# 67 of 367 transfers joined, and the planner's boxes of 16-bit tiles mended, in a two-layer spectral kernel

## The chip, the core and the metric

The kernel runs on one core of one Trainium2 chip. The metric is the device time of one execution in microseconds (us); the time before is the median of three runs. Engines are named as in the profile: PE (matrix multiply), PEld (its weight load), DVE (vector), ACT (scalar and activation), POOL (GpSimd), SP (issues transfers). SPq and ACTq are the issues of transfers by SP and ACT.

## The reference

x is one sequence of 2048 rows of 512 numbers. Four steps are added to it in turn, each on the layer-normalized x: layer A, layer B, layer A, layer B.

```
x = x + _A_ref(_layernorm(x, axis=-1), A_w_r, A_w_i)
x = x + _B_ref(_layernorm(x, axis=-1), B_A_re, ..., B_Dskip)
x = x + _A_ref(_layernorm(x, axis=-1), A_w_r, A_w_i)
x = x + _B_ref(_layernorm(x, axis=-1), B_A_re, ..., B_Dskip)
```

Layer A is a two-dimensional real Fourier transform over rows and columns, a product with a complex weight for each frequency, and the inverse transform. Layer B convolves every column with its own kernel of 2048 taps, by transforms of length 4096, and adds x times Dskip. The kernel of layer B is K[d, l] = Re sum over n of C B dt exp(dt A l), for 512 columns d and 128 states n; it depends on the parameters alone and is the same in both layers B.

## The kernel before, in words

Everything is float32 in matmuls, apart from bfloat16 factors for the exponentials. All transforms are written as small dense matmuls in two or three steps, with twiddle tables from the host. x (128 x 16 x 512) stays in SBUF, and large fixed areas (`Y`, `Ya`, `wk`, `apart`) are cut into rings of tiles by hand; a ring's line gives the number of columns and of tiles, `"KT": (512, 4)` for instance.

The work falls into two parts, each with a list of its own. The first part holds the first layer A (`forward_a`, `first_a` for 16 groups of frequencies, `inv_a` for 16 row blocks), the making of layer B's kernel K (`load_k`, `exp_k`, `unit_k` for 32 units, `store_k` for four quarters q), and the kernel's spectrum. That spectrum has two steps. `turn_k(q, i)` reads a piece of K back from the DRAM list `kd`, multiplies it with `cRk` (L1253) and stores both halves to the DRAM list `yk` (L1274, issued by ACT). `spectra_k(q)` reads `yk` (L837) with a table `cGk` (L834), multiplies (the matmuls of `spectrum`, L826), copies on ACT (L846) and stores to the DRAM list `khat` (L847, issued by ACT). It makes the first 256 of the 512 columns; the other 256 are made in the second part inside `group_b` (L898 reads `yk`, L907 stores `khat`), with blocks of the table that `load_g` loads (L866).

The second part holds the rest of the first layer B (`forward_b`, `group_b` for eight pairs of frequency groups and two column halves e, `inv_b`), the second layer A (`first_a` once, `group_a` 15 times) and the second layer B. The last quarter of K (q = 3) is turned here, from tiles of the rings `yk` and `gk` that `load_t` holds for it until its four turns are stored.

While `first_a` runs in the first part, its tables stand in x's own place (ring `G`, five tiles), so `inv_a` loads x's rows anew from DRAM (L732), as soon as all 16 groups are done.

What sets the order. Each piece of work is a generator. It yields what it needs next (an engine, tiles of a ring, the time of an event), and `Clock.run` takes the piece that can go first by planned times, ties by a rank written by hand. The planned times come from a cost table `COST` and from transfers' bytes through one rate; a planned instruction waits for earlier ones whose boxes (partitions and columns in a tensor) it meets. `Clock.boxes` works these boxes out. For a tile viewed as bfloat16 it counts the columns in 16-bit elements and leaves them so, though they are compared with columns of float32 tiles. Each engine then works off its own instructions in exactly this order; real waits are semaphores, put in from the real addresses.

Transfers go through two queues, SP's and ACT's. The built program has eight completion semaphores for them and gives them out in turn over the merged order of both queues. So that a semaphore is never in use twice, a transfer is issued only when the one eight places ahead has landed; the engine that issues it stands still until then.

```
yield "SP KT KT gb", self.after(("turn", 0), 8)
...
for j in range(2):
    nc.scalar.copy(kh[j].rearrange("p r d -> p (r d)"), p[j])
    nc.scalar.dma_start(self.khat[:, 2 * q + j, :, :256], kh[j])
```

The two loads of a table and of its weights stand next to each other at L595 and L597 (`group_a`) and at L667 and L669 (`first_a`); the products with the table are L623 and L685, those with the weights are on DVE.

Of the kernel before, what the change touches and what calls it, by code (L numbers as in the profile page):

```python
# [10 lines left out]
AF = mybir.ActivationFunctionType  # L11
OP = mybir.AluOpType

RING1 = {"yd": (1024, 5), "oh": (1280, 1), "KS": (2048, 1), "KT": (512, 4), "yh": (512, 4), "gb": (256, 3), "st": (256, 2), "sk": (128, 1)}
# [31 lines left out]
WORK = 17664  # L46
# [149 lines left out]
class Clock:  # L196
# [51 lines left out]
    @staticmethod  # L248
    def boxes(ap):

        if str(ap.space) == str(DRAM):
            return [(0, 1, 1, ap.offset, 1, ap.offset + sum(a * (b - 1) for a, b in ap.ap) + 1)]
        (s, n), *rest = ap.ap
        size = mybir.dt.size(ap.dtype) / mybir.dt.size(ap.tensor.dtype)
        width = round(int(np.prod(ap.tensor.shape[1:])) / size)
        p, o = divmod(ap.offset, width)
        rest = sorted(((a, b) for a, b in rest if b > 1 and a), key=lambda d: -abs(d[0]))
        o += sum(a * (b - 1) for a, b in rest if a < 0)
        rest = [(abs(a), b) for a, b in rest]
# [142 lines left out]
class Net:  # L402
# [185 lines left out]
    def group_a(self, g):  # L588

        nc = self.nc  # L590
# [4 lines left out]
        nc.sync.dma_start(ca, self.io["cGa"][g])  # L595
        W = G[:, 768:1796].rearrange("p (r s f) -> p r s f", r=2, s=2)
        nc.sync.dma_start(G[:, 768:1798], self.io["W"][g])  # L597
# [62 lines left out]
    def first_a(self, r, g):  # L660

        nc = self.nc
# [63 lines left out]
    def inv_a(self, r, s2, st):  # L726

        nc = self.nc
        xs = self.x[:, s2, :]
        yield "SP" if not r else "PE", self.after(("group", r), 16)  # L730
        if not r:
            nc.sync.dma_start(xs, self.io["A_x"].rearrange("b (p s) d -> p (b s) d", p=128)[:, s2, :])  # L732
            self.mark("again", s2)
            yield "+"
        yield "PE p:t y"
        Y4 = self.w("y", [128, 512])
# [25 lines left out]
        q = self.psum("h")  # L762
        nc.tensor.matmul(q, self.RaT, Y4, start=True, stop=True)
        self.drop(Y4)
        yield "DVE" if r else ("DVE", self.after(("again", s2)))

        two = xs.rearrange("p (a b) -> p a b", a=2)
        nc.vector.tensor_tensor(two, two, q[:, None, :256].to_broadcast([128, 2, 256]), op=OP.add)
# [60 lines left out]
    def spectra_k(self, q):  # L829

        nc = self.nc
        yield "SP KT KT gb", self.after(("turn", 0), 8)
        gb = self.w("gb", [128, 2, 4, 32])
        nc.sync.dma_start(gb, self.io["cGk"][q])  # L834
# [3 lines left out]
        yield "PE p:k yh yh"  # L838
        kh = [self.w("yh", [128, 2, 256]) for _ in range(2)]
        p = self.psum("k")  # L840
        p = p[:, :512], p[:, 512:]
        self.spectrum(gb, y, p)
        self.drop(gb, *y)
        yield "ACT"
        for j in range(2):
            nc.scalar.copy(kh[j].rearrange("p r d -> p (r d)"), p[j])  # L846
            nc.scalar.dma_start(self.khat[:, 2 * q + j, :, :256], kh[j])  # L847
        self.mark("khat", q)

    def tables(self, r):  # L850
# [7 lines left out]
            self.nc.sync.dma_start(self.gi[r, q], self.io["cGb"][q])  # L858
            self.mark("gi", r, q)

    def load_g(self, q):

        yield "SP gk", self.emitted(("rows", 0, 1), 8)
        gk = self.gk[q] = self.w("gk", [128, 2, 4, 32])
        self.timer.keep(gk)
        self.nc.sync.dma_start(gk, self.io["cGk"][q])  # L866
        self.mark("gk")
        yield self.emitted("gk", q + 1)

    def early(self, q):  # L870

# [337 lines left out]
    def load_t(self):  # L1209
# [11 lines left out]
        nc.sync.dma_start(self.sk3, self.io["B_Dskip"].rearrange("(q a d) -> q a d", q=4, a=1)[3])  # L1221
        self.mark("last")

    def turn_k(self, q, i):

        nc = self.nc
        kd = self.kd[q].rearrange("j (a s) d -> a j (s d)", s=16)
        last = q == 3
        if last:
            yield self.emitted("last")  # L1230
            KT = self.KT3[:, :, 128 * i:128 * i + 128]
        else:
            yield "SP KT", self.after(("stored", q))
            KT = self.w("KT", [128, 4, 128])
            nc.sync.dma_start(KT, kd[:, :, 128 * i:128 * i + 128])
        if i == 0:
            if last:
                sk = self.sk3
            else:
                yield "SP sk"  # L1240
                sk = self.w("sk", [1, 128])
                nc.sync.dma_start(sk, self.io["B_Dskip"].rearrange("(q a d) -> q a d", q=4, a=1)[q])
            yield ("DVE", self.after("last")) if last else "DVE"
            o = KT[0:1, :, 0:32]
            nc.vector.tensor_tensor(o, o, sk.rearrange("p (j d) -> p j d", j=4), op=OP.add)
        yield ("PE p:x p:x", self.after("last")) if last else "PE p:k"
        if last:
            p = [self.psum("x") for _ in range(2)]
        else:
            p = self.psum("k")  # L1250
            p = p[:, :512], p[:, 512:]
        for h in range(2):
            nc.tensor.matmul(p[h], self.Rk[:, h, :], KT if last else KT.rearrange("p j m -> p (j m)"), start=True, stop=True)  # L1253
        if not last:
            self.drop(KT)
        for h in range(2):
            if not last:
                yield "ACT yh"
                r = self.w("yh", [128, 4, 128])
            elif not h:  # L1260
                yield "ACT"
                r = KT
            else:
                yield "DVE"
                r = self.wk[:, self.own[2].offset % WORK + 512 * i:][:, :512].rearrange("p (s d) -> p s d", s=4)
            out, in_ = r.rearrange("p s (j d) -> p s j d", j=4), p[h].rearrange("p (j s d) -> p s j d", j=4, s=4)
            if last and h:
                nc.vector.tensor_copy(out, in_)
# [5 lines left out]
            nc.scalar.dma_start(self.yk[q // 2, :, :, :, i, h, 128 * (q % 2):128 * (q % 2) + 128]  # L1274
                                .rearrange("g c a d -> (g c) a d"), r)
            if not last:
                self.drop(r)
            yield "+"
        self.mark("turn", q // 2)
        if last:  # L1280
            self.left -= 1
            if not self.left:
                self.drop(*self.own)

    def plan_k(self):

        M, KS = {}, {}
        self.F, self.th = self.w("F", [128, 2, 2, 512]), self.w("th", [128, 512])
        self.hi = [self.w("hi", [128, 1024]).bitcast(BF).rearrange("p (a r m) -> p a r m", a=2, r=2) for p in range(3)]
        yield -130, self.setup_b()  # L1290
        yield -110, self.setup_a()
        for a in range(2):
            for r in range(2):
                yield -105, self.setup_f(a, r)
        for b in range(8):
            yield 4 * b - 2, self.load_k(b)
            for n in range(6):
                yield 4 * b - 1, self.exp_k(b, n, M)
            for u in range(4 * b, 4 * b + 4):
                yield u, self.unit_k(u, M, KS)  # L1300
# [87 lines left out]
    def plan_rest(self, sb):  # L1388
# [100 lines left out]
```

## Time and profile before

| | |
|---|---|
| median of 3 runs | 803.64 us (803.43 to 808.02) |
| the profiled execution | 801.81 us |
| its span, first to last instruction | 800.0 us |
| mean granted PE clock | 0.944 |
| transfers issued | 367 |

A line of the waits reads "who <- for whom: us in total, times, longest". A line of a timeline reads "start, length, engine, line, operation, output <- input, count", with the engine's idle time ahead of it and who ended it in brackets. A wait is put down to the event that came last. "L826" is line 826 of the kernel before. Tensors have the program's names without numbers, so a tile of a ring shows as the area that it is cut from (`wk`, `Y`, `Ya`, `x`).

### The profile page before, as it was taken

To read this page: it belongs to the slowest core of one execution; us is meant where nothing else is said; L and a number is where in the kernel's file an instruction comes from. 1 tells how busy PE (TensorE), PEld (TensorE's weight loads), DVE (VectorE), ACT (ScalarE), POOL (GpSimd) and SP (SyncE) were. 2 spreads that over 40 slices of the span, in tenths; PEclk is the share of its full clock that TensorE was granted. 3 is DMA by queue.
4 is the path that set the end of the run, shared out by engine and by line. 5 is a ranking of instruction groups with operands and counts; after the bars stand their busy time and mean duration, and the time that the engine had idled before them with its cause. 6 is when DMAs were issued, how large, how long until landed. Compare 5 with 4: busy or idle time off the path is not lost. (4 is left out here: it accounts for less than half of the span.)

```text
span 800.0 us, 23463 instructions
## 1 busy us (share of the span) xinstructions
PE 648.6 (81%) x9892; PEld 419.3 (52%) x9892; DVE 510.2 (64%) x1022; ACT 419.5 (52%) x767; POOL 306.5 (38%) x339
## 2 busy tenths in 40 slices
PE   4389888967899799888858887889887898788796
PEld 4377555535456344346423453777665554444465
DVE  5975667747748594885525454886767588466532
ACT  5765898886886957845232324175533233433130
POOL 4290336516425340320314325264544554075420
PEclk9699999997999999999898999999997999999999
DMA  9217212630624668547986783940664524866839
GB/s 325 60 59 274 89 47 84 192 96 14 217 80 151 233 205 244 181 133 165 259 219 194 193 246 131 255 174 1 232 218 139 186 56 107 186 195 160 257 89 281
DMA packets 85960, 132.51 MB, mean 166 GB/s; under 512 B 5756, under 2 KB 57728, under 8 KB 85216
## 3 DMA queue, kind: packets, MB, share of 16 engines
q1 hardware_dynamic: 51424, 93.26, 38.3%
q10 hardware_dynamic: 34432, 37.76, 16.6%
q8 instruction: 78, 1.28, 0.7%
q14 instruction: 26, 0.21, 0.1%
HBM read 70.31 MB, written 27.13 MB: 122 GB/s over the span
## 5 line engine op out<-in xcount | busy, mean ns | idle before, releaser
L1174 POOL TENSOR_TENSOR Y<-wk,Y 128x1024 f32<-128x1024 f32 x32 | 64.8, 2027 | 120.5 <-issue 70.6
L927 POOL TENSOR_TENSOR wk<-wk 128x512 f32<-128x512 f32 x32 | 40.0, 1274 | 111.5 <-DVE wk L921 110.4
L965 PE MATMUL ps<-wk,cRbT 64*128 64x256 f32 x512 | 61.4, 384 | 5.5 <-DMA wk<-Ya 3.5
L921 DVE TENSOR_TENSOR wk<-ps,Y 128x512 f32<-128x512 f32 x64 | 39.5, 682 | 40.7 <-PE ps L826 34.8
L795 ACT COPY wk<-ps 128x512 f32<-128x512 f32 x64 | 37.1, 587 | 52.7 <-PE ps L793 45.4
L1159 DVE SCALAR_TENSOR_TENSOR wk<-wk,ps 128x1024 f32<-128x1024 f32 x32 | 38.9, 1216 | 40.5 <-ACT wk L1157 40.4
L793 PE MATMUL ps<-wk,cRb 128*32 128x256 f32 x1024 | 60.1, 380 | 4.4 <-DVE wk L515 2.8
L1127 PE MATMUL ps<-wk,Y 96*128 96x512 bf16 x128 | 44.0, 422 | 24.1 <-DVE Y L1170 13.9
L938 PE MATMUL ps<-wk,Y 32*32 32x256 f32 x1344 | 40.0, 415 | 24.7 <-ACT Y L947 9.3
L965 PEld LDWEIGHTS ps<-wk,cRbT 64*128 64x128 f32 x512 | 51.8, 187 | 15.1 <-issue 5.6
L558 PE MATMUL ps<-cRa,wk 128*128 128x256 f32 x128 | 36.6, 411 | 28.1 <-POOL wk L540 24.8
L921 DVE TENSOR_TENSOR Y<-ps,wk 128x512 f32<-128x512 f32 x64 | 39.6, 683 | 26.1 <-issue 17.5
L793 PEld LDWEIGHTS ps<-wk,cRb 128*32 128x32 f32 x1024 | 37.9, 109 | 28.2 <-DVE wk L515 3.4
L1187 PEld LDWEIGHTS ps<-Y 128*32 128x32 f32 x2048 | 36.4, 125 | 27.8 <-issue 12.8
L1143 ACT ACTIVATE Y<-ps 128x1024 f32<-128x1024 f32 x48 | 46.3, 1030 | 7.3 <-PE ps L1127 7.1
L1187 PE MATMUL ps<-Y 128*32 128x64 f32 x2048 | 42.0, 243 | 9.1 <-ACT wk L676 2.5
L947 ACT COPY Ya<-ps 128x256 f32<-128x256 f32 x64 | 19.3, 385 | 56.5 <-PE ps L938 42.9
L1170 DVE TENSOR_TENSOR Y<-ps,Y 128x1024 f32<-128x1024 f32 x32 | 39.0, 1218 | 13.0 <-ACT ps L1163 12.9
L742 PE MATMUL ps<-cDaT,apart 128*32 128x256 f32 (+1 forms) x256 | 46.3, 328 | 0.5 <-DVE x L770 0.3
L971 DVE TENSOR_TENSOR x<-x,ps 128x256 f32<-128x256 f32 x64 | 24.8, 408 | 32.9 <-PE ps L965 32.8
L540 POOL TENSOR_TENSOR wk<-wk 128x256 f32<-128x256 f32 x32 | 25.9, 808 | 49.6 <-ACT wk L513 43.9
L927 POOL TENSOR_TENSOR wk<-Y 128x512 f32<-128x512 f32 x22 | 27.5, 1276 | 45.1 <-DVE Y L921 40.1
(218 smaller groups left out, 1649.9 us busy)
## 6 DMA issues: line engine op xcount, KB each, us to landing
yk<-wk ACTq DMA_DIRECT2D x32, 256.0 KB
wk<-khat SPq DMA_DIRECT2D x16, 512.0 KB
Y<-in_W_dram SPq DMA_DIRECT2D x12, 515.0 KB
x<-in_cPa_dram SPq DMA_DIRECT2D x16, 384.0 KB
Y<-in_cGa_dram SPq DMA_DIRECT2D x12, 384.0 KB
x<-in_W_dram SPq DMA_DIRECT2D x16, 258.0 KB
x<-in_A_x_dram SPq DMA_DIRECT2D x8, 512.0 KB
kd<-wk SPq DMA_DIRECT2D x4, 1024.0 KB
```

Source lines behind the costliest of these rows:

```text
L742: nc.tensor.matmul(p[32 * i:32 * i + 32, o:o + n], self.folded(r, i)[:, b, s2].rearrange("p g m -> p (g m)"), self.DaT[:, b, first:first + ...
L793: self.nc.tensor.matmul(p[o:o + 32, 256 * h:256 * h + 256], self.Rb[:, 2 * h + j, 32 * a:32 * a + 32], xn[s], start=True, stop=True)
L921: nc.vector.tensor_tensor(t[c][:, j], x, kh[:, j, ::-1, :] if c else kh[:, j], op=OP.mult)
L927: nc.gpsimd.tensor_tensor(Z[:, :, c], t[0][:, :, c], t[1][:, :, c], op=op)
L938: nc.tensor.matmul(v[j][h][i:i + 32], gi[o:o + 32, j, 4 + 2 * s + c, :], Z[o:o + 32, j, c, :], start=c == 0, stop=c == 1)
L965: nc.tensor.matmul(q[s], self.RbT[o, i, :], y[o, i, :], start=i == 0, stop=i == 3)
L1127: self.nc.tensor.matmul(p, f[:, c:c + 128], self.oh[:k, o:o + 512], start=True, stop=True)
L1143: nc.scalar.activation(m[:, :, 1024:] if i == 2 else m[:, i, :1024], p.rearrange("p (i m) -> p i m", i=2) if i == 2 else p, AF.Exp)
L1159: nc.vector.scalar_tensor_tensor(s, c, MAGIC, p, op0=OP.subtract, op1=OP.subtract)
L1170: nc.vector.tensor_tensor(E[:, 1, :1024], p, m[:, :1024], op=OP.mult)
L1174: nc.gpsimd.tensor_tensor(E[:, 0, :1024], c, m[:, :1024], op=OP.mult)
L1187: nc.tensor.matmul(pk[32 * j:32 * j + 32, 64 * e:64 * e + 64], E1[:, r, i, :], E2[:, r, i], start=r == 0, stop=r == 1)
```

## The change

Seven things. (1) The host joins each group's table and weights into one array (`GA`, `PA`), and `group_a` and `first_a` load each with one transfer: 32 fewer. (2) `spectra_k` loads the two `yk` groups with one transfer and stores the two `khat` groups with one, after both copies: 16 fewer. (3) `inv_a` reloads x's rows two by two: 8 fewer. (4) `load_g` loads the eight blocks as 4, 3 and 1, which needs that many neighbouring tiles at once: 5 fewer. (5) A new piece `load_kt` loads a piece of `kd` for two turns at a time, with rows of 256 numbers and not 128: 6 fewer. (6) The rings `KT` and `yh` have two tiles of 1024 columns and not four of 512; a turn takes one tile of `yh` for both halves. The stores to `yk` remain two per turn. (7) `Clock.boxes` counts the columns of every tile in 32-bit words.

```
-RING1 = {..., "KT": (512, 4), "yh": (512, 4), ...}
+RING1 = {..., "KT": (1024, 2), "yh": (1024, 2), ...}
...
         step = min([a for a, _ in rest], default=1)
+        size = mybir.dt.size(ap.dtype) / 4
...
-        nc.sync.dma_start(ca, self.io["cGa"][g])
+        nc.sync.dma_start(G, self.io["GA"][g])
...
-        nc.sync.dma_start(G[:, 768:1798], self.io["W"][g])
...
-        nc.sync.dma_start(ca, self.io["cPa"][g])
+        nc.sync.dma_start(G, self.io["PA"][g])
...
-        nc.sync.dma_start(W, self.io["W1"][g])
...
-        yield "SP" if not r else "PE", self.after(("group", r), 16)
-        if not r:
-            nc.sync.dma_start(xs, self.io["A_x"].rearrange("b (p s) d -> p (b s) d", p=128)[:, s2, :])
+        yield "SP" if not r and s2 % 2 == 0 else "PE", self.after(("group", r), 16)
+        if not r and s2 % 2 == 0:
+            two = slice(s2, s2 + 2)
+            nc.sync.dma_start(self.x[:, two, :], self.io["A_x"].rearrange("b (p s) d -> p (b s) d", p=128)[:, two, :])
...
-        yield "SP KT KT gb", self.after(("turn", 0), 8)
+        yield "SP KT gb", self.after(("turn", 0), 8)
...
-        y = [self.w("KT", [128, 2, 256]) for _ in range(2)]
-        for j in range(2):
-            nc.sync.dma_start(y[j], self.yk[0, 2 * q + j].rearrange("c a b h d -> (c a b) h d"))
+        y = self.w("KT", [128, 2, 2, 256])
+        nc.sync.dma_start(y.rearrange("p g h d -> p g (h d)"), self.yk[0, 2 * q:2 * q + 2].rearrange("g c a b h d -> (c a b) g (h d)"))
...
         for j in range(2):
-            nc.scalar.copy(kh[j].rearrange("p r d -> p (r d)"), p[j])
-            nc.scalar.dma_start(self.khat[:, 2 * q + j, :, :256], kh[j])
+            nc.scalar.copy(kh[:, j].rearrange("p r d -> p (r d)"), p[j])
+        nc.scalar.dma_start(self.khat[:, 2 * q:2 * q + 2, :, :256], kh)
...
-    def load_g(self, q):
-
-        yield "SP gk", self.emitted(("rows", 0, 1), 8)
...
+    def load_g(self, q, n):
+
+        yield "SP" + " gk" * n, self.emitted(("rows", 0, 1), 8)
...
+        self.nc.sync.dma_start(self.wk[:, o:o + 256 * n].rearrange("p (q m) -> p q m", q=n),
+                               self.io["cGk"][q:q + n].rearrange("q p a b m -> p q (a b m)"))
...
+    def load_kt(self, q, i):
+
+        nc = self.nc
+        yield "SP KT", self.after(("stored", q))
+        t = self.kt[q, i] = self.w("KT", [128, 4, 256])
+        self.timer.keep(t)
+        nc.sync.dma_start(t, self.kd[q].rearrange("j (a s) d -> a j (s d)", s=16)[:, :, 256 * i:256 * i + 256])
+        if i == 0:
+            yield "+SP sk"
+            self.sk[q] = self.w("sk", [1, 128])
+            self.timer.keep(self.sk[q])
+            nc.sync.dma_start(self.sk[q], self.io["B_Dskip"].rearrange("(q a d) -> q a d", q=4, a=1)[q])
+        self.mark("kt", q, i)
...
-                yield "ACT yh"
-                r = self.w("yh", [128, 4, 128])
+                yield "ACT" if h else "ACT yh"
+                y = y if h else self.w("yh", [128, 2, 4, 128])
+                r = y[:, h]
...
                 for i in range(4 if b < 7 else 0):
+                    if i % 2 == 0:
+                        yield 4 * b + 6 + i, self.load_kt(b // 2, i // 2)
                     yield 4 * b + 6 + i, self.turn_k(b // 2, i)
...
-        for q in range(8):
-            yield 0, self.load_g(q)
+        for q, n in ((0, 4), (4, 3), (7, 1)):
+            yield 0, self.load_g(q, n)
```

More of the change, by code (lines that the diff above doesn't have):

```diff
@@ L12 @@
 OP = mybir.AluOpType
-RING1 = {"yd": (1024, 5), "oh": (1280, 1), "KS": (2048, 1), "KT": (512, 4), "yh": (512, 4), "gb": (256, 3), "st": (256, 2), "sk": (128, 1)}
+RING1 = {"yd": (1024, 5), "oh": (1280, 1), "KS": (2048, 1), "KT": (1024, 2), "yh": (1024, 2), "gb": (256, 3), "st": (256, 2), "sk": (128, 1)}
 RINGW = {"y": (514, 2), "d": (258, 3), "c": (256, 3), "a": (512, 2)}
@@ L729, in inv_a @@
         xs = self.x[:, s2, :]
-        yield "SP" if not r else "PE", self.after(("group", r), 16)
-        if not r:
-            nc.sync.dma_start(xs, self.io["A_x"].rearrange("b (p s) d -> p (b s) d", p=128)[:, s2, :])
-            self.mark("again", s2)
+        yield "SP" if not r and s2 % 2 == 0 else "PE", self.after(("group", r), 16)
+        if not r and s2 % 2 == 0:
+            two = slice(s2, s2 + 2)
+            nc.sync.dma_start(self.x[:, two, :], self.io["A_x"].rearrange("b (p s) d -> p (b s) d", p=128)[:, two, :])
+            self.mark("again", s2 // 2)
             yield "+"
@@ L764, in inv_a @@
         self.drop(Y4)
-        yield "DVE" if r else ("DVE", self.after(("again", s2)))
+        yield "DVE" if r else ("DVE", self.after(("again", s2 // 2)))
         two = xs.rearrange("p (a b) -> p a b", a=2)
@@ L831, in spectra_k @@
         nc = self.nc
-        yield "SP KT KT gb", self.after(("turn", 0), 8)
+        yield "SP KT gb", self.after(("turn", 0), 8)
         gb = self.w("gb", [128, 2, 4, 32])
         nc.sync.dma_start(gb, self.io["cGk"][q])
-        y = [self.w("KT", [128, 2, 256]) for _ in range(2)]
-        for j in range(2):
-            nc.sync.dma_start(y[j], self.yk[0, 2 * q + j].rearrange("c a b h d -> (c a b) h d"))
-        yield "PE p:k yh yh"
-        kh = [self.w("yh", [128, 2, 256]) for _ in range(2)]
+        y = self.w("KT", [128, 2, 2, 256])
+        nc.sync.dma_start(y.rearrange("p g h d -> p g (h d)"), self.yk[0, 2 * q:2 * q + 2].rearrange("g c a b h d -> (c a b) g (h d)"))
+        yield "PE p:k yh"
+        kh = self.w("yh", [128, 2, 2, 256])
         p = self.psum("k")
         p = p[:, :512], p[:, 512:]
-        self.spectrum(gb, y, p)
-        self.drop(gb, *y)
+        self.spectrum(gb, [y[:, j] for j in range(2)], p)
+        self.drop(gb, y)
         yield "ACT"
         for j in range(2):
-            nc.scalar.copy(kh[j].rearrange("p r d -> p (r d)"), p[j])
-            nc.scalar.dma_start(self.khat[:, 2 * q + j, :, :256], kh[j])
+            nc.scalar.copy(kh[:, j].rearrange("p r d -> p (r d)"), p[j])
+        nc.scalar.dma_start(self.khat[:, 2 * q:2 * q + 2, :, :256], kh)
         self.mark("khat", q)
@@ L859, in tables @@
             self.mark("gi", r, q)
-    def load_g(self, q):
-        yield "SP gk", self.emitted(("rows", 0, 1), 8)
[L864 to L868, printed above, removed]
+    def load_g(self, q, n):
+        yield "SP" + " gk" * n, self.emitted(("rows", 0, 1), 8)
+        t = [self.w("gk", [128, 2, 4, 32]) for _ in range(n)]
+        o = t[0].offset % WORK
+        for i in range(n):
+            self.gk[q + i] = t[i]
+            self.timer.keep(t[i])
+            assert t[i].offset % WORK == o + 256 * i
+        self.nc.sync.dma_start(self.wk[:, o:o + 256 * n].rearrange("p (q m) -> p q m", q=n),
+                               self.io["cGk"][q:q + n].rearrange("q p a b m -> p q (a b m)"))
+        for _ in range(n):
+            self.mark("gk")
+        yield self.emitted("gk", q + n)
     def early(self, q):
@@ L1222, in load_t @@
         self.mark("last")
+    def load_kt(self, q, i):
[10 more added lines that the diff above has]
+        self.mark("kt", q, i)
     def turn_k(self, q, i):
         nc = self.nc
-        kd = self.kd[q].rearrange("j (a s) d -> a j (s d)", s=16)
         last = q == 3
[L1229 to L1235, printed above, removed]
-        if i == 0:
[L1237 to L1244, printed above, removed]
+        came = "last" if last else ("kt", q, i // 2)
+        yield self.emitted(came)
+        KT = self.KT3[:, :, 128 * i:128 * i + 128] if last else self.kt[q, i // 2][:, :, 128 * (i % 2):128 * (i % 2) + 128]
+        if i == 0:
+            yield "DVE", self.after(came)
+            o, sk = KT[0:1, :, 0:32], self.sk3 if last else self.sk[q]
             nc.vector.tensor_tensor(o, o, sk.rearrange("p (j d) -> p j d", j=4), op=OP.add)
-        yield ("PE p:x p:x", self.after("last")) if last else "PE p:k"
+            if not last:
+                self.drop(sk)
+        yield "PE p:x p:x" if last else "PE p:k", self.after(came)
         if last:
@@ L1252, in turn_k @@
         for h in range(2):
-            nc.tensor.matmul(p[h], self.Rk[:, h, :], KT if last else KT.rearrange("p j m -> p (j m)"), start=True, stop=True)
-        if not last:
-            self.drop(KT)
+            nc.tensor.matmul(p[h], self.Rk[:, h, :], KT, start=True, stop=True)
+        if not last and i % 2:
+            self.drop(self.kt[q, i // 2])
         for h in range(2):
             if not last:
-                yield "ACT yh"
-                r = self.w("yh", [128, 4, 128])
+                yield "ACT" if h else "ACT yh"
+                y = y if h else self.w("yh", [128, 2, 4, 128])
+                r = y[:, h]
             elif not h:
@@ L1275, in turn_k @@
                                 .rearrange("g c a d -> (g c) a d"), r)
-            if not last:
-                self.drop(r)
+            if not last and h:
+                self.drop(y)
             yield "+"
@@ L1287, in plan_k @@
         M, KS = {}, {}
+        self.kt, self.sk = {}, {}
         self.F, self.th = self.w("F", [128, 2, 2, 512]), self.w("th", [128, 512])
@@ L1475 @@
     arrays = {"A_x": np.ascontiguousarray(A_x), "B_Dskip": np.ascontiguousarray(B_Dskip),
-              "W": host_w(A_w_r, A_w_i), "W1": host_w1(A_w_r, A_w_i),
               **host_k(B_A_re, B_A_im, B_B_re, B_B_im, B_C_re, B_C_im, B_log_dt),
               **tables_a(), **tables_b(), **table_k()}
+    for name, table, w in (("GA", "cGa", host_w(A_w_r, A_w_i)), ("PA", "cPa", host_w1(A_w_r, A_w_i))):
+        arrays[name] = np.concatenate([arrays.pop(table).reshape(16, 128, 768), w.reshape(16, 128, -1)], 2)
     nc = bacc.Bacc("TRN2", target_bir_lowering=False, num_devices=1, dynamic_dma_scratch_size=4096)
```

## The prediction

> **What bounds the kernel now.** I read the page first, then the busy time by stage, the waits, and last the timeline of each queue around the transfers that the change joins.
>
> ```profile
> PE 648.6 (81%) x9892; PEld 419.3 (52%) x9892; DVE 510.2 (64%) x1022; ACT 419.5 (52%) x767; POOL 306.5 (38%) x339
> ...
> DMA packets 85960, 132.51 MB, mean 166 GB/s; under 512 B 5756, under 2 KB 57728, under 8 KB 85216
> ```
> ```profile
> 55.00:80.00 25.00, 22.26 (x158) 18.69 (x159) 15.85 (x26) 15.46 (x32) 5.05 (x7) 1.00 0.78 265
> 80.00:253.00 173.00, 142.84 (x2000) 90.93 (x1998) 119.72 (x183) 141.19 (x169) 77.96 (x57) 0.92 0.33 102
> 253.00:345.00 92.00, 79.00 (x1256) 38.77 (x1248) 63.87 (x114) 68.51 (x86) 29.45 (x20) 0.96 0.66 211
> ...
> 376.00:432.00 56.00, 42.50 (x754) 22.03 (x745) 22.03 (x43) 16.23 (x36) 11.59 (x10) 0.85 0.84 219
> ```
> PE is busy for 81% of the span and is the bound on average; the rest is waiting inside a fixed order of work. By stage (columns: stretch, length, then PE, PEld, DVE, ACT, POOL busy, granted clock, DMA share, GB/s): from 80 to 253 us PE and ACT are both near 82%, with the DMA engines at 0.33; from 376 to 432 us PE is busy for only 42.50 of 56 and the DMA share is 0.84. A transfer's speed is therefore no bound over the span. What can matter is who stands still until a transfer may be issued.
>
> That is to be seen here. The program has eight completion semaphores for its transfers and hands them out in turn, over both issuing queues, so a transfer waits until the one eight places ahead of it in the list has landed, and the engine that issues it waits with it. These rows are waits of that kind, since the data of the two has nothing to do with each other (ACT stores the kernel's spectra to khat while SP reloads x):
>
> ```profile
> ACT wk L846 <- DMA x<-in_A_x_dram: 2.4, 2, 1.9
> ACT wk L1157 <- DMA x<-in_A_x_dram: 2.2, 1, 2.2
> ```
> ```profile
> SPq L732 <- DMA khat<-wk: 4.4, 2, 3.8
> ```
> The Trainium skill says the same of the place of such a wait (DMA: Bandwidth & Descriptors, Anatomy of one DMA): the DMA engines never wait on a semaphore, the issuing sequencer does before dispatch; the trace agrees, in the 2.4 us above. Joining transfers does not make bytes fewer. It puts more bytes into eight places, and it brings the transfer eight places ahead further back in time.
>
> **The change, part by part.** The sum is made against the profiled execution, 801.81 us with a span of 800.0; it stands 1.83 us under the median of the three runs (803.64), and I add that at the end.
>
> *Blocks of the kernel's table (8 loads to 3).* The one large stall that a join can reach lies here.
>
> ```profile
> 408.33 0.54 ACTq L1274 DMA_DIRECT2D yk<-wk  x1
> 408.94 0.68 ACTq L811 DMA_DIRECT2D Ya<-wk  x1
> 418.84 0.53 ACTq L1274 DMA_DIRECT2D yk<-wk  x1
> 419.41 1.20 ACT L947 COPY Y<-ps 128x256 f32<-128x256 f32 x4 [10.50 <-DMA Ya<-wk]
> ```
> ```profile
> 409.61 1.98 PE L1253 MATMUL ps<-wk,cRk 128*128 128x512 f32 x4
> 419.92 2.91 PE L938 MATMUL ps<-wk,Y 32*32 32x256 f32 x64 [8.33 <-ACT Y L947]
> ```
> ```profile
> 411.63 0.69 DVE L1268 COPY wk<-ps 128x512 f32<-128x512 f32 x1 [2.71 <-PE ps L1253]
> ```
> ```profile
> 411.56 2.83 SPq L866 DMA_DIRECT2D wk<-in_cGk_dram  x3
> 432.26 0.38 SPq L898 DMA_DIRECT2D wk<-yk  x1
> 432.73 1.84 SPq L866 DMA_DIRECT2D wk<-in_cGk_dram  x4
> ```
> ACT's yk store is issued at 418.84, although ACT was through with the issue before it at 408.94 + 0.68 = 409.62, and what it stores was written by DVE at 411.63 + 0.69 = 412.32 at the latest. It waits for the Ya store of 408.94, eight places ahead; three of those places are the block loads of 411.56. PE stands behind ACT's copies for 8.33 us. Three blocks are loaded early and four late because only three of the seven slots are free before the last turn is stored; I take it that the join of three (blocks 4 to 6) keeps the first place and the join of four the second. Then two places fall away, the store's forerunner becomes one that SP issued before 408, and the store can go when its data is there: 418.84 - 412.4 = 6.4 us earlier. The store after the next one then meets the landing of the same Ya store, but what ACT does behind it waits for the 2.91 us of L938 on PE anyway, so I take 6.0 of the 6.4. Bounds: 0, if another long transfer comes to stand eight places ahead, and the whole wait, 418.84 - 409.62 = 9.2. Block 0 now comes with the late four, together with three others. Its reader:
>
> ```profile
> 444.62 1.96 PE L826 MATMUL ps<-wk 64*32 64x256 f32 x32
> ```
> It starts 10 us after the last of the four is issued (432.73 + 1.84), so the cover holds, even with PE 6 us earlier, since the yk load that gates it moves with it. Cost 0. **Term A: -6.0 (0 to -9.2).**
>
> *Spectra (16 loads of yk to 8, 16 stores of khat to 8) and x's rows (16 reloads to 8).*
>
> ```profile
> 332.16 0.57 ACT L846 COPY wk<-ps 128x512 f32<-128x512 f32 x1
> 332.76 0.37 ACTq L847 DMA_DIRECT2D khat<-wk  x1
> 333.22 0.59 ACT L846 COPY wk<-ps 128x512 f32<-128x512 f32 x1 [0.49 <-ACT wk L846]
> ```
> Between the two copies of a pair ACT loses 0.49 us to the store's issue; eight of these go: 8 x 0.49 = 3.9 us. The three waits on x's reload above sum to 2.4 + 2.2 = 4.6 us; of these about 3 x 0.49 are the issues themselves, so 3.1 more go when the reload takes eight places and not sixteen. Together 7.0 us of ACT. ACT is not busy for 92 - 68.51 = 23.5 us of this stage, so they are 30% of its gaps. PE waits for ACT in it as follows (its own rows; the weight loads overlap):
>
> ```profile
> PE ps L1187 <- ACT wk L746: 1.3, 1, 1.3
> PE ps L1127 <- ACT Y L1143: 1.3, 1, 1.3
> ...
> PE ps L763 <- ACT wk L746: 1.0, 2, 0.7
> ```
> 30% of 3.6 us is 1.1; I take 1.5, because DVE and POOL wait for ACT as well. Bounds 0 and 7.0. The reload itself:
>
> ```profile
> 269.71 14.36 SPq L732 DMA_DIRECT2D x<-in_A_x_dram  x16
> 284.11 0.90 SPq L834 DMA_DIRECT2D wk<-in_cGk_dram  x1
> ```
> ```profile
> 281.21 0.69 DVE L768 TENSOR_TENSOR x<-x,ps 128x512 f32<-128x512 f32 x1 [0.55 <-PE ps L763]
> ```
> SP is held for 14.36 us by sixteen issues. With eight it is free some us earlier, and what is queued behind (a table, yk and the list kd) starts earlier. The first pair lands later than the first row did, but its reader DVE starts 11.5 us after the issue and waits for PE. Both taken as 0. **Term B: -1.5 (0 to -7.0).**
>
> *Layer A's tables with weights (32 pairs to 32 single loads).* Bytes are the same; what PE needs first now comes together with the weights, so up to one weight transfer later.
>
> ```profile
> 560.31 0.33 SPq L595 DMA_DIRECT2D Y<-in_cGa_dram  x1
> 560.74 0.71 SPq L597 DMA_DIRECT2D Y<-in_W_dram  x1
> ```
> ```profile
> 573.07 1.03 PE L623 MATMUL ps<-Ya,Y 128*128 128x257 f32 x4
> ```
> The load issued at 560.31 is the first that goes into a slot given back; PE reads it 12.8 us later, and the slots ahead are the cover. If they ran out, the price would be a weight transfer per group. Taken as 0, as are SP's 32 issues of 0.3 to 0.7 us, since SP waits for slots and not for its own time. In the first layer the five joined loads stand ahead of the factors' stores on SP:
>
> ```profile
> 63.19 1.96 SPq L1013 DMA_DIRECT2D spe<-Y  x3
> ```
> Five places fewer, the same bytes: between -2 (all of these 1.96) and 0, taken as 0, because the stores still queue behind the same bytes.
>
> *The list kd (12 loads to 6), rings of half as many tiles of twice the size.*
>
> ```profile
> 142.62 2.04 SPq L1235 DMA_DIRECT2D wk<-kd  x4
> ```
> ```profile
> 149.82 1.98 PE L1253 MATMUL ps<-wk,cRk 128*128 128x512 f32 x4
> ```
> ```profile
> wk<-kd SPq DMA_DIRECT2D x12, 256.0 KB
> ...
> wk<-in_cGk_dram SPq DMA_DIRECT2D x16, 128.0 KB
> ```
> The first turn waits for 512 KB and not 256 KB. PE comes to it 7.2 us after the first issue, so the second load's issue, 0.5 us later, is under cover. A slot of yh now comes back when both stores of a turn have landed; two turns fit, as before. Cost 0, at most one issue of 0.5 us for each of the three groups, 1.5.
>
> *Mended boxes, and the new pieces in the list.* No instruction by themselves. They can change the order on each engine; this is the slower rival's place.
>
> **Sum:** 801.81 - 6.0 - 1.5 = 794.3; with 1.83 for the median, 796.1. I predict 796.
>
> **The rivals.**
>
> *Hidden: nothing moves.* The waits are part of a list that is laid out anew; another transfer comes to stand eight places ahead, and ACT's gaps are filled by waits for PE. For it: ACT is busy for only 68.51 of 92 us. Against: the 10.50 us wait has one cause with a known place. Terms A and B at 0 give 803.6. A rule of the Trainium skill ends there as well (DMA: Bandwidth & Descriptors, Rules for kernel authors): it asks to coalesce, but sees mostly overhead only under 64 KB. The smallest joined loads are those of 128 KB, so by that rule alone the sum would be 803.6; whether the trace agrees the result alone can show.
>
> *Slower: the new order opens holes.* An engine works off its list in order, and the order is computed from costs, not from what happens.
>
> ```profile
> 160.00:180.00 20.00, 12.82 (x114) 6.27 (x103) 9.39 (x15) 16.99 (x20) 3.64 (x3) 0.91 0.31 96
> ...
> 280.00:300.00 20.00, 19.42 (x310) 9.51 (x308) 18.07 (x37) 10.14 (x14) 8.21 (x6) 0.92 0.63 205
> ```
> From 80 to 345 us PE idles (173 - 142.84) + (92 - 79.00) = 43.2 us of 265, 3.3 in 20; the slices run from 20 - 19.42 = 0.6 to 20 - 12.82 = 7.2, and the worst is that of the first group of turns. A hole of that depth costs 7.2 - 3.3 = 3.9 us. One each at the four places with new pieces (two later groups of turns, spectra, reload) costs 15.6: 796.1 + 15.6 = 811.7. It decides from the second hole on (7.8 over the 7.5 gained). For it: joined loads bring two turns at once. Against: the same order could close holes as well.
>
> *More: both terms at their ends.* 9.2 + 7.0 = 16.2 give 801.81 - 16.2 + 1.83 = 787.4. For it: PE's idle time from 376 to 432 us is 13.5, so it has room. Against: DVE and PE take over as the wait, as the 412.32 above.
>
> **How the numbers follow.** Forecast 0.38 (own range 792 to 800), hidden 0.20 (800 to 806), slower 0.22 (807 to 818), more 0.20 (782 to 792). The range 786 to 812 leaves out about half of each outer case, together 2 in 10. Within 1% is about what a measurement of this kernel can tell from no change; 1% of 803.64 is 8.0, so the bounds are 795.6 and 811.7. Faster by over 1%: the whole of "more" and somewhat under half of the forecast, 0.37. Slower: most of that rival, 0.17. Within: the rest, 0.46.
>
> **What would show it.** Term A: ACT's gap of 10.50 us ahead of L947 shrinks to about 4, and PE's 8.33 to about 2. Term B: one khat store per pair, no ACT wait on x's reload, SP through with the reload before 282 us. Tables: no PE wait on them. The slower rival: PE's idle time from 80 to 345 us above 43 us by more than 8. The prediction is wrong if a join's later landing shows as a PE wait, or if the stage up to 345 us is longer than before.

## The result, and the profile after

| | before | after |
|---|---|---|
| median (20 runs of each) | 803.34 us | 795.9 us |
| the profiled execution | 801.81 us | 791.16 us |
| its span | 800.0 us | 789.4 us |
| its mean granted clock | 0.944 | 0.942 |

The ratio is 0.9911, with a 95% interval of 0.9884 to 0.9937; a second measurement gave 0.9947 (0.9914 to 0.998; medians 797.29 to 801.89). By the two ratios the change is worth 4 to 7 us, by their intervals 2 to 9. Ratios here are over each kernel's runs within 1.5% of its fastest; where that leaves few runs, the medians of all stand beside it.

The page of the changed kernel, engines and DMA (busy us, share, count), answers to the first fence of the prediction:

```profile
PE 649.1 (82%) x9892; PEld 417.1 (53%) x9892; DVE 505.8 (64%) x1022; ACT 419.4 (53%) x768; POOL 304.6 (39%) x339
...
DMA packets 76696, 132.50 MB, mean 168 GB/s; under 512 B 4684, under 2 KB 53584, under 8 KB 75952
```

The work is the same; 9264 packets fewer carry the same bytes. By stage (stretch, length, PE, PEld, DVE, ACT, POOL busy, clock, DMA share, GB/s):

```profile
80.00:253.00 173.00, 145.27 (x2000) 92.37 (x1999) 119.05 (x184) 141.48 (x170) 77.47 (x57) 0.89 0.32 101
253.00:345.00 92.00, 85.18 (x1414) 42.13 (x1417) 66.87 (x126) 70.36 (x89) 29.95 (x21) 0.96 0.63 212
...
376.00:432.00 56.00, 44.69 (x995) 21.95 (x985) 24.71 (x41) 18.17 (x48) 20.00 (x16) 0.94 0.90 236
```

From 80 to 345 us PE idles (173 - 145.27) + (92 - 85.18) = 34.6 us and not 43.2, so the changed kernel shows no new hole there. (The same 92 us hold 1414 matmuls after and 1256 before, so the two rows are not the same piece of work.) The timeline of ACT around the blocks' loads:

```profile
402.02 0.54 ACTq L1285 DMA_DIRECT2D yk<-wk  x1
402.63 0.78 ACTq L811 DMA_DIRECT2D Ya<-wk  x1
406.37 0.53 ACTq L1285 DMA_DIRECT2D yk<-wk  x1
406.95 1.20 ACT L952 COPY Y<-ps 128x256 f32<-128x256 f32 x4 [4.35 <-DMA Ya<-wk]
```
```profile
407.46 2.91 PE L943 MATMUL ps<-wk,Y 32*32 32x256 f32 x64 [2.18 <-ACT Y L952]
```

ACT's gap of 10.50 us is 4.35, PE's 8.33 is 2.18. The yk store goes at 406.37, and it still waits for a place. It stores DVE's half of the second turn, and the timelines of DVE, before and after, have that half written by 408.92 and by 402.62:

```profile
408.24 0.68 DVE L1268 COPY wk<-ps 128x512 f32<-128x512 f32 x1
```
```profile
401.94 0.68 DVE L1279 COPY wk<-ps 128x512 f32<-128x512 f32 x1
```

So before, the data was there ahead of ACT, which was free at 409.62, and the whole 9.2 us up to 418.84 were a wait for the place. After, ACT is free at 402.63 + 0.78 = 403.41, and the transfer now eight places ahead, a Ya store that SP issued at 398.64, landed at 406.30 by the trace's semaphore events: 3.0 us of waiting are left. Behind it ACT stands twice more for a place, 2.1 and 2.0 us, in the timeline of ACT and, with PE waiting behind it, in that of PE:

```profile
410.78 3.00 ACTq L1285 DMA_DIRECT2D yk<-wk  x2
```
```profile
415.57 1.96 PE L826 MATMUL ps<-Y 64*32 64x256 f32 x64 [1.88 <-ACT wk L1281]
```

The spectra have one store for two copies, and SP issues the reload in 4.19 us and not 14.36; the transfer behind it, however, goes only 2.7 us earlier than before. The timelines of ACT and of SP:

```profile
277.05 1.07 ACT L845 COPY wk<-ps 128x512 f32<-128x512 f32 x2
278.15 0.37 ACTq L846 DMA_DIRECT2D khat<-wk  x1
```
```profile
266.63 4.19 SPq L732 DMA_DIRECT2D x<-in_A_x_dram  x8
281.37 0.33 SPq L834 DMA_DIRECT2D wk<-in_cGk_dram  x1
```

SP stands from 270.82 to 281.37. Eight places ahead is the khat store that ACT issued at 269.41, now joined to 512 KB; by the trace's semaphore events it landed at 281.35. From the first issue of the reload to the transfer behind it takes 14.74 us, before 14.40, so the 2.7 us come from a reload that begins 3.1 us earlier.

### The profile page after: what moved, and what is told of

It reads as the page before. It is cut to its first block, busy times and chain, and to the rows that moved or that the text cites. A ratio compares the mean times of both kernels' runs of the same rounds, so it can differ in the third digit from the quotient of the medians.

```text
span 789.4 us, 23363 instructions
## 1 busy us (share of the span) xinstructions
PE 649.1 (82%) x9892; PEld 417.1 (53%) x9892; DVE 505.8 (64%) x1022; ACT 419.4 (53%) x768; POOL 304.6 (39%) x339
## 3 DMA queue, kind: packets, MB, share of 16 engines
q8 instruction: 78, 1.28, 0.7%
## 5 line engine op out<-in xcount | busy, mean ns | idle before, releaser
L970 PE MATMUL ps<-wk,cRbT 64*128 64x256 f32 x512 | 64.1, 398 | 8.4 <-DMA wk<-Ya 5.7
L970 PEld LDWEIGHTS ps<-wk,cRbT 64*128 64x128 f32 x512 | 54.1, 196 | 18.8 <-issue 8.5
L926 DVE TENSOR_TENSOR Y<-ps,wk 128x512 f32<-128x512 f32 x64 | 39.5, 684 | 25.8 <-issue 18.0
L793 PEld LDWEIGHTS ps<-wk,cRb 128*32 128x32 f32 x1024 | 33.8, 111 | 34.8 <-ACT wk L795 3.7
L932 POOL TENSOR_TENSOR wk<-Y 128x512 f32<-128x512 f32 x22 | 27.5, 1275 | 45.6 <-DVE Y L926 33.3
```

The source lines that it names most:

```text
L793: self.nc.tensor.matmul(p[o:o + 32, 256 * h:256 * h + 256], self.Rb[:, 2 * h + j, 32 * a:32 * a + 32], xn[s], start=True, stop=True)
L926: nc.vector.tensor_tensor(t[c][:, j], x, kh[:, j, ::-1, :] if c else kh[:, j], op=OP.mult)
L932: nc.gpsimd.tensor_tensor(Z[:, :, c], t[0][:, :, c], t[1][:, :, c], op=op)
L970: nc.tensor.matmul(q[s], self.RbT[o, i, :], y[o, i, :], start=i == 0, stop=i == 3)
```

## The experiments

Each of the change's parts was built alone, or taken out of the whole. The parts: g, the blocks' loads as 4, 3 and 1; s, spectra, kd and the rings KT and yh; b, the mended boxes; x, the rows two by two; p, layer A's tables with weights. The right-hand columns are durations in each kernel's profiled execution, read off the timelines: T, SP's first to its third store to kd (two groups of turns); R, its third to its fourth store (the reload and what lies around it); F, from there to ACT's first `Ya<-wk` store (in the forward transform of layer B); A, ACT's fourth `Ya<-wk` to its first `wk<-Y` (the blocks' stretch); L, from there to its eighth `khat<-Y` (the stretch behind).

| kernel | parts | median, before | ratio (95%) | T | R | F | A | L |
|---|---|---|---|---|---|---|---|---|
| before | none | | | 128.9 | 85.3 | 29.8 | 36.2 | 46.9 |
| after | all | 795.90, 803.34 | 0.9911 (0.9884-0.9937) | 124.0 | 84.0 | 28.0 | 26.7 | 51.7 |
| e1 | g | 800.30, 803.59 | 0.9969 (0.9936-1.0002) | 128.1 | 84.5 | 29.9 | 26.4 | 50.9 |
| e2 | s | 812.03, 803.59 | 1.0128 (1.0072-1.0183) | 123.1 | 97.9 | 27.7 | 36.0 | 48.5 |
| e3 | b | 802.12, 803.59 | 0.9973 (0.9934-1.0012) | 128.3 | 85.2 | 29.9 | 36.5 | 48.4 |
| e4 | x | 802.70, 803.59 | 0.9966 (0.9924-1.0009) | 128.1 | 84.5 | 30.1 | 33.2 | 47.4 |
| e5 | all but b | 809.48, 801.88 | 1.0074 (1.0031-1.0118) | 123.1 | 96.3 | 27.6 | 29.3 | 49.7 |
| e6 | s, b | 801.30, 801.88 | 1.0013 (0.9975-1.0050) | 124.7 | 85.5 | 27.5 | 34.7 | 46.9 |
| e7 | p | 801.93, 801.88 | 1.0012 (0.9975-1.0049) | 132.8 | 84.8 | 29.8 | 33.6 | 47.7 |
| e8 | g, padded | 805.52, 801.88 | 1.0060 (1.0018-1.0101) | 127.6 | 84.5 | 29.8 | 32.1 | 49.0 |
| e9 | all but g | 798.84, 801.89 | 0.9854 (0.9797-0.9911) | 125.3 | 87.2 | 27.8 | 33.1 | 47.9 |
| e10 | b, g, x | 800.74, 801.89 | 1.0010 (0.9972-1.0048) | 124.6 | 86.2 | 29.9 | 28.0 | 52.7 |
| e11 | all, again | 797.29, 801.89 | 0.9947 (0.9914-0.9980) | 125.2 | 83.9 | 27.8 | 30.8 | 49.3 |
| e12 | all but x | 794.89, 801.89 | 0.9913 (0.9872-0.9954) | 126.9 | 87.2 | 27.5 | 28.1 | 49.4 |

e9's ratio rests on three of its twelve runs, one at 783.65 us; its medians give 798.84 / 801.89 = 0.9962.

**e1, the blocks alone.**

```
-        for q in range(8):
-            yield 0, self.load_g(q)
+        for q, n in ((0, 4), (4, 3), (7, 1)):
+            yield 0, self.load_g(q, n)
```

> The kernel before with one part of the change alone: the eight loads of the kernel's table blocks joined as 4, 3 and 1. Theory (the place eight ahead): two places fall away between the Ya store and the yk store, ACT's stall of 10.50 us ahead of the copies of the first group of layer B shrinks to about 4, and the time falls by 6.0 us, ratio 0.9925 (797.3 us). Rival (the whole gain of the change is the order of the list and the stores elsewhere): the stall moves to another transfer, ratio 1.000 within 0.003.

0.9969: 2.5 us where 6.0 were expected, with an interval that just reaches 1. Yet the stall ahead of the copies shrinks as foretold. The timeline of ACT in e1:

```profile
404.94 0.69 ACTq L811 DMA_DIRECT2D Ya<-wk  x1
407.86 0.53 ACTq L1280 DMA_DIRECT2D yk<-wk  x1
408.43 1.20 ACT L953 COPY Y<-ps 128x256 f32<-128x256 f32 x4 [3.52 <-DVE wk L1274]
...
410.28 5.10 ACTq L1280 DMA_DIRECT2D yk<-wk  x2
415.42 1.20 ACT L953 COPY Y<-ps 128x256 f32<-128x256 f32 x4 [5.30 <-DVE wk L927]
```

The gap is 3.52 us. But the stall is divided more than it is gone. By the semaphore events the store of 407.86 still stands 2.2 us, for the Ya store that SP issued at 401.31, and the second of the two stores from 410.28 stands 4.1 us for the old Ya store of 404.94; PE idles 3.24 us behind that. Over the whole stretch from the fourth Ya store to the first `wk<-Y`, ACT stands for places 7.0 us on average in the six kernels with g and 9.4 in the seven without.

**e8, the same with the places filled up.** Five transfers of 512 bytes to an unused list stand behind the joined loads. PE, DVE, ACT and POOL have exactly e1's order.

```
+        for i in range(1, n):
+            self.nc.sync.dma_start(self.pad[q + i:q + i + 1], self.io["B_Dskip"].rearrange("(q a d) -> q a d", q=4, a=1)[0])
```

> The blocks joined as 4, 3 and 1 as in the first experiment, with five transfers of 512 bytes more behind the joined loads (two behind the three, three behind the four), so that as many transfers stand in the list as before; the order of all other engines is that of the first experiment. Theory (the place eight ahead): the yk store meets the Ya store again, ACT's wait ahead of the copies of the first group of layer B is about 10 us again where the first experiment had 3.52, and the time is that of the kernel before, ratio 1.000. Rival (larger transfers are what helps, or the changed order): the wait stays at 3.5 us and the ratio at 0.997.

The wait is back to the tenth of a microsecond. The timeline of ACT in e8:

```profile
407.80 0.67 ACTq L811 DMA_DIRECT2D Ya<-wk  x1
417.63 0.53 ACTq L1282 DMA_DIRECT2D yk<-wk  x1
418.20 1.20 ACT L955 COPY Y<-ps 128x256 f32<-128x256 f32 x4 [10.43 <-DMA Ya<-wk]
...
452.70 5.62 ACTq L965 DMA_DIRECT2D wk<-Y  x2
458.42 1.20 ACT L955 COPY Ya<-ps 128x256 f32<-128x256 f32 x4 [11.11 <-PE ps L946]
459.98 1.07 ACT L914 COPY Y<-ps 128x512 f32<-128x512 f32 x2 [0.36 <-PE ps L826]
465.94 0.37 ACTq L915 DMA_DIRECT2D khat<-Y  x1
```

The bytes of the blocks come in as few transfers as in e1, and the wait is that of before, 10.43 beside 10.50 us. What counts is the number of places, not the size. The five small transfers cost (1.0060 - 0.9969) x 803 = 7.3 us, some 4 us more or less by the two intervals; in the two profiles the stretches A and L together are 3.8 us longer (81.1 and 77.3). The Trainium skill (DMA: Bandwidth & Descriptors, Rules for kernel authors) asks to coalesce many small transfers and sees mostly overhead under 64 KB; of loads of 128 KB that rule says nothing. Here the trace shows another price beside overhead, the place: 10.43 us of wait with the five transfers, 3.52 without.

And e8 is slower than the kernel before, by 0.6% (4.8 us), though its places at the blocks are the same. What differs besides is the order: where the joined loads take several slots at once, 64 of PE's L938 matmuls (numbered as before) and ACT's four copies of them fall behind the second pair of `wk<-Y` stores. The timeline of ACT before, then after:

```profile
455.20 1.20 ACT L947 COPY Ya<-ps 128x256 f32<-128x256 f32 x4 [2.10 <-PE ps L938]
460.45 4.42 ACTq L957 DMA_DIRECT2D wk<-Y  x2
```
```profile
445.21 4.20 ACTq L962 DMA_DIRECT2D wk<-Y  x2
450.78 1.20 ACT L952 COPY Ya<-ps 128x256 f32<-128x256 f32 x4 [14.08 <-PE ps L943]
```

In this order the pair and the khat store behind it come early enough to meet the transfers eight places ahead. Ahead of each store of the pair ACT stands some 3 to 4 us in the kernels without g as well, but there an event of PE ends the wait. In e8 and e1 an event of PE still ends the first of these waits. The place ends the second, 1.2 and 1.5 us behind the event of PE, and it alone holds the khat store, 4.8 us in e8 and 1.8 in e1; in the seven kernels without g no place holds any of the three.

A is 28.2 us on average in the six kernels with g and 34.8 in the seven without, 6.5 less, of which 5.5 are idle time of PE. L is 50.6 and 47.7, 2.9 more. (e8 is in neither.) That these places make L longer is not shown: in the changed kernel they cost 0.1 us there, and its L is 51.7; and of the 2.9 us, PE's idle time is 0.9 and its busy time 2.0, for the same matmuls. Nor does e8's profile show the 4.8 us: its A and L together are 81.1 us, the average without g is 82.4. So what makes e8 slower than the kernel before stays open. A joined load with the order of before was not tried.

**e9, the change without the blocks.**

> The changed kernel with the eight loads of the table's blocks single again. Theory (the place eight ahead): ACT's wait of about 9 us behind the Ya store is back and costs the 6.0 us of the prediction, ratio to the kernel before 0.9911 + 0.0075 = 0.9986. Rival (the blocks are worth only what they gave alone, 0.3%): 0.994.

The timeline of ACT in e9 has that wait once more:

```profile
404.15 0.76 ACTq L811 DMA_DIRECT2D Ya<-wk  x1
414.79 0.53 ACTq L1279 DMA_DIRECT2D yk<-wk  x1
415.36 1.20 ACT L946 COPY Y<-ps 128x256 f32<-128x256 f32 x4 [11.24 <-DMA Ya<-wk]
```

The wait is confirmed. The time, by the medians 0.9962 beside 0.9943 of e11 on the same chip, loses 1.5 us without the blocks, nearer the rival's 0.3% than the theory's 6.0 us; but e9's runs lie between 783.65 and 807.35 us and settle little.

**e2, spectra alone.**

```
-"KT": (512, 4), "yh": (512, 4)
+"KT": (1024, 2), "yh": (1024, 2)
...
-        yield "SP KT KT gb", self.after(("turn", 0), 8)
+        yield "SP KT gb", self.after(("turn", 0), 8)
```

> The kernel before with the spectra's part alone: yk loads and khat stores of a pair joined, the list kd loaded for two turns at a time, rings KT and yh with two tiles of 1024. Theory: ACT loses 8 x 0.49 us less to issues, of which 30% count, so about -1 us, ratio 0.9985. Rival (the order of the turns changes as well, and the 3 us that the changed kernel gained up to 267 us come from it): about -4 us, ratio 0.995.

Both were wrong: slower by 1.28%. The waits of e2 from 253 to 345 us, then its timelines of SP and of DVE:

```profile
DVE wk L1247 <- DMA wk<-kd: 13.2, 1, 13.2
```
```profile
266.43 15.31 SPq L732 DMA_DIRECT2D x<-in_A_x_dram  x16
...
282.78 0.41 SPq L1229 DMA_DIRECT2D wk<-kd  x1
```
```profile
276.17 0.68 DVE L1170 SCALAR_TENSOR_TENSOR Y<-ps,Y 128x512 f32<-128x512 f32 x1
290.05 0.28 DVE L1247 TENSOR_TENSOR wk<-wk 1x128 f32<-1x128 f32 x1 [13.20 <-DMA wk<-kd]
```

DVE's list has the addition of Dskip to a loaded piece of kd next after 276.85 us. That load stands on SP behind the reload, and DVE, with everything behind the addition, waits 13.2 us for an instruction of 0.28 us.

**e3, the mended boxes alone.**

```
         step = min([a for a, _ in rest], default=1)
+        size = mybir.dt.size(ap.dtype) / 4
```

> The kernel before with the mended boxes alone: no transfer is changed, only the order in which instructions are listed (on ACT and PE, in the first 300 us). Theory: an order as good as before, 0 us, ratio 1.000. Rival: the 3 us gained up to 267 us in the changed kernel come from this, ratio 0.996.

0.9973, and its interval holds both. Alone it can't be told from nothing.

**e6, spectra and boxes together, and e5, the change without the boxes.**

> The kernel before with the spectra's part and the mended boxes together. Theory (the loss of the spectra's part is the one hole that the order opens, and the mended boxes close it): 1.0128 - 13.2 / 803 = 0.9964, between 0.993 and 1.000. Rival (the joined loads of kd themselves make PE wait, in each group of turns): the loss stays, 1.008 to 1.013.

> The changed kernel without the mended boxes: all joins as in it, the list of instructions between 253 and 345 us as in the spectra's part alone, where DVE stood 13.2 us for the list kd behind x's reload. Theory (the mended boxes take that hole out of the list): the hole of about 13 us is back, and the ratio to the kernel before is 0.991 + 13 / 803 = 1.007 (1.002 to 1.010). Rival (the hole was there because SP issued sixteen row reloads ahead of kd; with eight it is gone in any order): 0.991.

1.0013 and 1.0074: both tell for the theory. e6 lies 0.0013 above the theory's range, and its interval (0.9975 to 1.0050) leaves out the rival's; that e5 meets the forecast to the third digit is luck, with an interval of 0.0043 to either side. In e5 the reload is in eight transfers, and the hole is there all the same, so it is the order and not the sixteen issues. (SP stands there 11.1 us for the joined khat store before it comes to kd.) The waits of e5 in the same stretch:

```profile
DVE wk L1252 <- DMA wk<-kd: 11.8, 1, 11.8
```

In the changed kernel the same addition is listed eleven microseconds of DVE's work later, and doesn't wait, though its load goes no earlier (283.11 after, 281.98 in e5). In e6 2.3 us of the wait are left. The timeline of DVE after:

```profile
287.99 0.18 DVE L492 BATCH_NORM_AGGREGATE mv<-st 128x2 f32<-128x6 f32 x1
288.10 0.28 DVE L1253 TENSOR_TENSOR wk<-wk 1x128 f32<-1x128 f32 x1
```

In the table R is 97.9 and 96.3 us in e2 and e5, and 85.2 on average in the other twelve. So the mended boxes, which change no transfer, take 11.9 us out of the change; by the ratios of e5 and the two of the whole it is 10 to 13. Why the corrected boxes lead the planner to this order was not traced.

Without the hole the spectra's part gains in one stretch. T is 124.6 us on average in the seven kernels with s and 127.6 in the others without e7, whose profile had the lowest clock (0.924); PE's idle time in T is 17.7 to 19.5 us with s and 20.4 to 22.1 without, e7 included. F looks shorter, 27.7 and 29.9, but that is no gain: PE runs 398 matmuls in it with s and 432 without, the rest falls into R. The stretch from the first to the fourth `Ya<-wk` store, which the table leaves out, is 27.6 us with s and 25.8 without. R, F and that stretch together are 141.0 us in the five kernels with s and b, and 140.7 in the seven without s. So about 3 us of gain are left, in T. e6 as a whole does not show them (1.0013), and the runs don't settle that.

**e4 and e12, the rows alone, and the change without them.**

```
-            nc.sync.dma_start(xs, self.io["A_x"].rearrange("b (p s) d -> p (b s) d", p=128)[:, s2, :])
+            nc.sync.dma_start(self.x[:, two, :], self.io["A_x"].rearrange("b (p s) d -> p (b s) d", p=128)[:, two, :])
```

> The kernel before with x's rows reloaded two by two alone: the order on PE, DVE, ACT and POOL stays as it was, only SP's list changes. Theory: the three ACT waits on x's reload (4.6 us) go, 30% of 3.1 us count, -1 us, ratio 0.999. Rival (SP is free some 7 us earlier and what stands behind it starts earlier, up to the khat stores' own waits): -3 us, ratio 0.996.

> The changed kernel with x's rows reloaded one by one again; the order on PE, DVE, ACT and POOL stays that of the changed kernel. Theory (ACT's khat stores meet the reload's places again, about 3 us as in the rows alone, 0.3%): 0.9945. Rival (the spectra's joined stores have made the waits rare, or the 0.3% of the rows alone was scatter): 0.991.

0.9966 alone, with 1 in its interval, and 0.9913 without the rows beside 0.9947 with them. The rows bring nothing that can be seen, and the change without them is as fast.

**e7, tables and weights.**

```
-        nc.sync.dma_start(ca, self.io["cPa"][g])
+        nc.sync.dma_start(G, self.io["PA"][g])
```

> The kernel before with layer A's tables joined with their weights alone; the order on PE, DVE, ACT and POOL stays as it was. Theory (the slots ahead cover the load): 0 us, ratio 1.000 within 0.002. Rival (32 places fewer let the loads of tables and the stores around them go earlier; the changed kernel gained 3 us between 560 and 645 us): -3 us, ratio 0.996.

1.0012: as predicted, nothing.

**e10 and e11, three parts, and the whole again.**

> The kernel before with three parts: mended boxes, blocks as 4, 3 and 1, x's rows two by two; spectra, kd and layer A's tables as before. Theory (the parts add up, and spectra and tables bring nothing): 0.9973 x 0.9969 x 0.9966 = 0.9908, as fast as the changed kernel. Rival (the changed kernel's gain needs the spectra's part with its 8 x 0.49 us of ACT): 0.995 or above.

> The changed kernel once more, as the measure for the other three on the same chip: 0.9911 (0.988 to 0.994) to the kernel before.

e10 is 1.0010, against 0.9947 for the whole on the same chip. The parts do not add up: what e10 lacks, the spectra's part and the tables, counts beside the others, and since the tables alone bring nothing it is likely the spectra's part. No kernel beat the changed one by a margin that can be measured.

## Why the prediction was right, and where it was not

The time was right: 796 forecast, 795.9 the median, and 797.29 the second time. Its composition was not, so that the two agree to 0.1 us is luck.

*Term A (-6.0).* The place was right, and so were the signs: gaps of 4.35 and 2.18 us where "about 4" and "about 2" were foretold, 6.5 us less in the stretch A, and e8 brings the wait back with nothing but places. The Trainium skill (DMA: Bandwidth & Descriptors, Why a DMA increments its semaphore by 16 and not by 1) asks for one semaphore for each transfer in flight; the trace agrees with how the program does it, eight in turn, and e8 shows what that costs. Three steps failed. First, the prediction took 412.32 for the end of the store's data. That is DVE's copy for the next turn, whose matmuls start at 409.61; the store's own data was there at 408.92, and in e1 the store goes at 407.86 while the later copy still runs (407.64 + 0.69). So the 6.4 us did not come from the data: the place took 9.2 us before and takes 3.0 after, and that the difference is near 6.4 is luck. Second, it took the next meeting with the old Ya store as covered by L938; it costs ACT 4.1 us and PE 3.24 in e1, and 2.0 and 1.88 in the changed kernel. Third, it ended the term there. It wrote that new pieces in the list "can change the order on each engine" and priced that at nothing in the sum; with g the stretch behind is 2.9 us longer, for a reason that is not shown. In time the blocks are worth 1.5 to 2.5 us by e9's medians and e1's ratio, with an uncertainty at least as large.

*Term B (-1.5).* The signs that it named came: one store per pair, no ACT wait on x's reload, SP through before 282 us. PE's own waits for ACT from 253 to 345 us, 3.6 us before, sum to 0.3 to 1.0 in the five kernels with s and b, and to 3.3 to 4.9 in all others. So the waits go, by more than the 1.5 us; but R, F and the stretch behind are no shorter for it (141.0 and 140.7 us). The step from PE's waits to the time failed. Alone the spectra cost 1.28%. And "what is queued behind starts earlier" failed: the reload frees SP 13.3 us earlier, and the joined khat store eight places ahead holds it 10.5 us. Here the join that frees the queue also makes a transfer that lands later for somebody. The gain that there was lay in T, about 3 us, which the term did not name.

*The list kd (0, at most 0.5 for each group).* No joined load of it was waited for by PE in the changed kernel. With the unmended order DVE waited 11.8 to 13.2 us for one.

*The mended boxes (0).* This was the largest omission: 11.9 us beside the spectra's part. The prediction put boxes and pieces into one rival, "the new order opens holes", with the reload among its four places. The place was right, but the two work against each other: the pieces open the hole, the boxes close it. Its depth, 3.9 us taken from a slice's idle time, was a third of the 11.9 measured.

*Tables (0).* Right.

*The rivals.* "Hidden" and "slower" did not come about for the whole; "slower" did in e5, 1.0074, by one hole and not four. "More" needed both terms at their ends; neither got there.

What stays open: the parts alone (e1, e6, e4, e7) multiply to 0.9960, with an uncertainty of 0.0075 from their four intervals, so that 0.9911 and 0.9947 are no contradiction. The runs show where one wait went and where one hole came from; what makes up the whole gain of 4 to 7 us is not shown.

## What to carry to other kernels

Where few completion semaphores go round over two queues, find for each stalled issue the transfer that many places ahead: a join can be worth what it does to such pairs, and it moves all others. Compare the order of the instructions on each engine before pricing a change in a planned list, since one instruction of 0.28 us listed ahead of its load cost 12 us. Read the data of a stalled store from its own copy before crediting the wait to data or place. Try a part both alone and taken out of the whole: here the spectra's part alone cost 1.28%, and the kernel without it and the tables (e10) was slower than the whole.

## What the hardware showed

The scatter of a kernel's time goes with the granted clock of TensorE: over the 29 runs of the kernel before beside e1 to e4, a straight line gives 4.4 us for 0.01 of mean clock, over the 35 beside e5 to e8 it gives 6.8, and in e9 the fastest run (783.65 us) had 0.953 and the slowest (807.35 us) 0.928. Two profiles of the same program, after and e11, differ by 789.4 to 795.2 us at clocks of 0.942 and 0.938, so a gain of 3 us read off one pair of profiles is no gain yet. The averages over many kernels' profiles above were needed for that reason.
